# Moving TensorE filler matmuls and two weight loads in a fused recurrence and soft mixture-of-experts kernel

## The chip, the cores and the metric

The kernel runs on one core of a Trainium2 chip. Its time is that of the device, in microseconds, as the median over several runs. One execution is also profiled; the profile's own times are counted from the start of its span. The engines are named as in the profile: PE (TensorE matmuls), PEld (its weight loads), DVE (VectorE), ACT (ScalarE), POOL (GpSimd) and SP (SyncE, which only issues transfers here).

## The reference

Two stages follow each other. The first is a gated linear recurrence over 5056 steps, for 4 batches and 256 channels; the second is a soft mixture of experts with 8 experts of 4 slots each over all 20224 tokens.

```python
# first stage, x and f_logit are [4, 5056, 256]
sig = 1.0 / (1.0 + np.exp(-f_logit))
f = lower_bound + (1.0 - lower_bound) * sig
i = 1.0 - f
for t in range(S):
    h = f[:, t] * h + i[:, t] * x[:, t]
    y[:, t] = h
# second stage, x is y as [20224, 256]; phi [256, 32], w1 [8, 256, 1024], w2 [8, 1024, 256]
logits = x @ phi
d = softmax of logits over all tokens
slot_input = (d.T @ x).reshape(8, 4, 256)
slot_out[e] = np.maximum(slot_input[e] @ w1[e], 0.0) @ w2[e]
c = softmax of logits over the slots
out = c @ slot_out
```

The dispatch softmax runs over all tokens, so no expert can start before the recurrence has ended, and no output can be written before the last expert is done. The inputs are 41.4 MB of x and f_logit and 16.8 MB of weights in float32; the output is 20.7 MB.

## The kernel before

**Units.** The sequence is cut into 10 groups of 512 steps (the ninth of 448). A unit is one group of one batch, so there are 40 units, numbered so that `n // 4` is the group and `n % 4` the batch. The loop at L425 walks through them. For a unit, `load` (L174) issues the transfers of f_logit and x on SP's queue six units ahead; `gate` (L192) computes the sigmoid on ACT; `enter` (L202) multiplies it with x on POOL into `u_t`; `s_to_channels` and `u_to_channels` transpose both into PSUM on PE; `decay` (L242) makes the factor `a` on ACT; `scan` (L253) runs the recurrence on DVE; `to_tokens` (L266) transposes the result back on PE into `hp`; and `keep_tokens` copies it to `ht`, on DVE or ACT.

**Groups.** Two groups at a time, `logits` multiplies with phi, `exps` (L308) takes the exponential on ACT, `weights_to_tokens` (L315) transposes it on PE into `ep` and copies it on DVE into `et`, and `slots` (L348) accumulates the slot inputs. With blocks of eight units, the exponential of a pair of groups comes at a unit with `n % 8 == 1`, its transposes at the end of the next unit, its first `slots` at the end of the one with `n % 8 == 3`.

**The order is written by hand.** The schedule is manual (L143), so each engine executes its instructions in the order of the program text. An engine that waits holds up everything behind it on that engine.

**Fillers.** `idle` (L163) issues matmuls on PE whose result nobody reads; they write the second half of the slot bank. They stand in the loop behind `u_to_channels` (L473 to L476). `spin` (L135) does the same later on, with a weight as operand and `tail` as destination. `rs_ps`, which holds the row sums of the combining softmax, is another part of `tail`.

**Weights.** `load_w` (L128) issues one expert weight on POOL's queue, converting float32 to bfloat16: 1 MB read, 512 KB written. The first eight are `w1_sb` (L130), the others `w2_sb` (L132). `W_AT` (L141) says behind which unit's `enter` how many are issued; the issues share POOL with `enter`, in order.

**Experts and output.** After the recurrence, `sin` (the normalised slot input) goes through w1 for all experts (`hi_ps`, L559), transposes (`ht_ps`), w2 for experts 0 to 3 (L595) and for 4 to 7 (L605). Experts 4 to 7 are one block of eight matmuls each, which waits for its `w2_sb`. Between the second and third block stand the remaining row sums and `SPINS` spins (L612 to L618). Then `slot_out` (L619) is scaled on DVE, `slot_bd` made on POOL, and the output stage multiplies, scales on DVE and ACT, and stores on SP's queue.

Of the kernel before, what the change touches and what calls it, by code (L numbers as in the profile page):

```python
# [18 lines left out]
def kernel(  # L19
# [10 lines left out]
    nc = tc.nc  # L30
    B, S, D = x.shape
    E = moe_w1.shape[0]
    F = moe_w1.shape[2]
    NS = moe_phi.shape[1]
    SPE = NS // E
    P = 128
# [5 lines left out]
    n_unit = n_grp * B  # L42
# [27 lines left out]
    ident = consts.tile([P, P], BF16, name="ident")  # L70
# [13 lines left out]
    def rep_constants(b):  # L84
        blk = ident_f[ds(b * NS, NS), ds(b * NS, NS)]
        nc.gpsimd.tensor_copy(rep[ds(b * NS, NS)], blk.unsqueeze(1).broadcast_to([NS, B, NS]))
# [48 lines left out]
    def spin(dst, k, w):  # L135
        for _ in range(k):
            nc.tensor.matmul(dst[:, ds(0, w)], w1_sb[0][:, 0, :P], w1_sb[0][:, 0, :w],
                             start=True, stop=True, skip_group_check=True)

    SPINS = 28  # L140
    W_AT = {17: 1, 25: 1, 30: 1, 31: 1, 32: 1, 33: 2, 34: 1, 36: 8}  # L141
    w_next = [0]
    ctx.enter_context(tc.manual_schedule())  # L143

# [3 lines left out]
    with tc.tile_pool(name="sp2", bufs=3) as sp2, \  # L148
# [9 lines left out]
        slot_bank = pslot.tile([P, 2, D], F32, name="slot_ps")  # L158
        slot_ps = slot_bank[:, 0]

        rep_bf = rep.rearrange("p b s -> p (b s)").bitcast(BF16)

        def idle(k, first=False):  # L163
            for i in range(k):
                nc.tensor.matmul(slot_bank[:, 1], ident, rep_bf,  # L165
                                 start=first and i == 0, stop=False, skip_group_check=True)
        xs, fs, sts, uts, pss, psus, hs, hps, hts, lgs, ets = ({} for _ in range(11))

        def tokens(src, n, k):
# [22 lines left out]
        def gate(n, k=2):  # L192
            if n % 2 == 0:
                sts[n // 2] = sp2.tile([P, 2, R, D], BF16, name="s_t", tag="s_t")
            s_t, f_t = sts[n // 2][:, ds(n % 2, k)], fs[n // 2][:, ds(n % 2, k)]
            if n // B == odd:
                m = (R + R3) * D
                s_t = s_t.rearrange("p u r d -> p (u r d)")[:, :m]
                f_t = f_t.rearrange("p u r d -> p (u r d)")[:, :m]
            nc.scalar.activation(s_t, f_t, ACT.Sigmoid, scale=-1.0)  # L200
# [27 lines left out]
        def s_to_channels(n):  # L228
            if n % 2 == 0:
                pss[n // 2] = psp.tile([P, 2, P, R], F32, name="sp", tag="sp")  # L230
            to_channels(n, pss[n // 2][:, n % 2], sts[n // 2][:, n % 2],
                        sts[n // 2][:, 0, R3])
# [31 lines left out]
        SINGLE = 6  # L264
# [28 lines left out]
        def batch_of(g):  # L293
            return [g & ~1, g | 1] if g < n_grp - 2 else [g]
# [64 lines left out]
        def unit(f, m):  # L359
            if 0 <= m < n_unit:  # L360
                f(m)
# [5 lines left out]
        def batch(f, m, i):  # L367
            m -= i
            if 0 <= m < n_unit and m % B == B - 1:
                gs = batch_of(m // B)  # L370
                if m // B == gs[-1] and i < len(gs):
                    f(gs[i])
# [52 lines left out]
        for n in range(n_unit):  # L425
            if n < SINGLE - 2:
                if n:
                    unit(to_tokens, n - 1)
                    unit(u_to_channels, n + 1)
                s_to_channels(n + 2)  # L430
                if n + 3 < SINGLE:
                    gate(n + 3, 1)
                decay(n + 2, 1)
                if n + 3 == SINGLE:
                    gate(n + 3)
                if n % 2 == 0:
                    unit(load, n + AHEAD)
                unit(enter, n + 3)
                rep_constants(n)
            else:  # L440
                end = n >= n_unit - 6
                if n % 2 == 0:
                    unit(load, n + AHEAD)
                    if n == SINGLE - 2:
                        to_tokens(n - 1)
                        keep_tokens(n - 1)
                    if not end:
                        unit(gate, n + 4)
                else:
                    unit(decay, n + 1)  # L450
                    if n == n_unit - 5:
                        gate(n + 3)
                        exps(odd - 1)
                if not end and n != n_unit - 7:
                    group(exps, n - 2)

                unit(enter, n + 3)
                for _ in range(W_AT.get(n, 0)):
                    load_w(w_next[0])
                    w_next[0] += 1  # L460

                if n == n_unit - 2:
                    unit(u_to_channels, n + 1)
                if n != SINGLE - 2:
                    unit(to_tokens, n - 1)
                if n == n_unit - 2:
                    keep_tokens(n - 1)
                if n % 2 == 0:
                    unit(s_to_channels, n + 2)
                    unit(s_to_channels, n + 3)  # L470
                if n != n_unit - 2:
                    unit(u_to_channels, n + 1)
                if n in (n_unit - 5, n_unit - 4):  # L473
                    idle(4)
                elif SINGLE - 2 < n < n_unit - 4 and n % (2 * B) in (1, 2, 5, 6, 7):
                    idle(5, n == SINGLE - 1)  # L476
                if n == n_unit - 2:
                    tail = psp.tile([P, 2, G], F32, name="tail", tag="sp")
                    rs_ps = tail[:, 0, ds(0, n_grp * R * B)].rearrange(
                        "p (q b) -> p q b", b=B)  # L480
                    late_ps, odd_ps = (
                        tail[:, 1].bitcast(BF16)[:, ds(i * R * P, R * P)].rearrange(
                            "p (r s) -> p r s", r=R) for i in range(2))
                    logits(odd)
                    exps(odd)
                    slots(odd - 1)
                    spin(tail[:, 1], 1, G)
                    odd_weights()
                elif not end:
                    group(logits, n - 1)  # L490
            if n == n_unit - 1:
                logits(last, [0, 1, 2])
                late_exps([0, 1, 2])
                row_sums(0)
                late_weights([0, 1, 2], nc.scalar.copy)

            unit(scan, n)
            if n not in (SINGLE - 2, n_unit - 2):
                unit(keep_tokens, n - 1)
            if n == n_unit - 3:  # L500
                weights_to_tokens(odd - 1)
                slots(odd - 2)
            elif not n >= n_unit - 6:
                group(weights_to_tokens, n - 3)
                batch(slots, n - 4, 0)
                batch(slots, n - 4, 1)
        hid, wide = (ld.tile([P, 2, R, D], F32, name=i, tag="x_t") for i in ("hid", "wide"))
        hid = hid.rearrange("p u r d -> p (u r d)").bitcast(BF16)[:, ds(0, FC * E // 2 * NS)]
        wide = wide.rearrange("p u r d -> p (u r d)").bitcast(BF16)[:, ds(0, FC * E // 2 * P)]
# [19 lines left out]
        for o in range(DC):  # L529
            nc.tensor.matmul(sin_ps[:, o], slot_v[:, o], rep[:, 0],  # L530
                             start=True, stop=True, skip_group_check=True)

    with tc.tile_pool(name="ew", bufs=1) as ew, \
# [18 lines left out]
        for q in range(E // Q):  # L552
            hi = ew.tile([P, F], BF16, name=f"hi{q}")
            for k in range(2):
                hi_ps = (psu.tile([P, H], F32, name="hi_ps", tag="up") if q == 0 else
                         pbig.tile([P, H], F32, name="hi_ps", tag=f"hi_ps{k}"))
                for o in range(DC):
                    for j in range(Q):
                        nc.tensor.matmul(hi_ps[ds(j * NS, NS)], sin[:, o],  # L559
                                         w1_sb[q * Q + j][:, o, ds(k * H, H)],  # L560
                                         start=(o == 0), stop=(o == DC - 1),
                                         skip_group_check=True)
# [30 lines left out]
        for e in range(Q):  # L593
            for fc in range(FC):
                nc.tensor.matmul(so4_ps[ds(fc % 4 * NS, NS), :], hid[:, fc, e],  # L595
                                 w2_sb[e][:, fc],
                                 start=(e == 0 and fc < 4),
                                 stop=(e == Q - 1 and fc >= FC - 4),
                                 skip_group_check=True)
# [3 lines left out]
        for j in range(Q):  # L603
            for fc in range(FC):
                nc.tensor.matmul(so_ps, wide[:, fc, j].rearrange("p b s -> p (b s)"),  # L605
                                 w2_sb[Q + j][:, fc],
                                 start=j == 0 and fc == 0, stop=j == Q - 1 and fc == FC - 1,
                                 skip_group_check=True)
            if j == 0:
                nc.tensor.matmul(so_ps, rep2, so4, start=False, stop=False,  # L610
                                 skip_group_check=True)
            if j == 1:  # L612
                for i in range(1, len(blocks)):
                    row_sums(i)
                q = n_grp * R - 1
                spin(tail[:, 1], SPINS, NS)
                nc.vector.reciprocal(rrow[:, wide_r:q], rs_ps[:, wide_r:q])
                nc.vector.reciprocal(rrow[:, q, ds(0, B // 2)], rs_ps[:, q, ds(0, B // 2)])  # L618
        nc.vector.tensor_scalar_mul(slot_out, so_ps, rcs)  # L619
        for u in range(2):  # L620
            nc.gpsimd.tensor_scalar_mul(slot_bd[:, u], slot_out, parity[:, ds(u, 1)])  # L621
# [139 lines left out]
```

## Time and profile before

| what | value |
|---|---|
| median of 7 runs | 202.17 us (201.5 to 205.59) |
| the profiled execution's own time | 203.09 us |
| its span | 201.3 us |
| mean granted clock of PE | 0.847 |
| PE, DVE, ACT, POOL busy | 71%, 71%, 68%, 51% of the span |
| queue of SP's loads and stores | 62.13 MB, 75.7% of the 16 DMA engines' span |
| queue of POOL's weight loads | 8.42 MB written, 21.2% of the 16 DMA engines' span |
| filler matmuls, L165 | 108, 273 ns each |
| spin matmuls, L137 | 73 |

The busy shares are averages over stages that differ: up to about 130 us the recurrence, to 147 us the experts, then the output. [...] A DMA share above 1 comes from packets of one engine that overlap. GB/s counts bytes written, so a weight load shows half of what it reads.

### The profile page before, as it was taken

Reading aid. Unit: us, or ns where it says so; the run is one execution under the profiler, and the core shown is the slowest. Engines: PE = TensorE matmul, PEld = TensorE weight load, DVE = VectorE, ACT = ScalarE, POOL = GpSimd, SP = SyncE. Lnnn points to the kernel's source line nnn. Section 1 sums busy time; section 2 is a strip of 40 time slices with the busy share of each in tenths; the row PEclk is TensorE's granted clock in tenths of the full one; section 3 lists DMA queues with packets and bytes.
Section 4 is the critical chain, followed back from the end, with each engine's and each line's share of the span. In section 5 each row is a group of like instructions: output and inputs, shape, how many; then the busy total and the mean of one; then the engine's idle time right before and its main releaser. Section 6 shows DMA issues by size and latency. Waiting matters only on the chain.

```text
span 201.3 us, 3263 instructions
## 1 busy us (share of the span) xinstructions
PE 143.8 (71%) x1201; PEld 104.9 (52%) x1201; DVE 142.7 (71%) x164; ACT 137.8 (68%) x194; POOL 101.9 (51%) x76
## 2 busy tenths in 40 slices
PE   0588585895878789785988778996779999970000
PEld 0367454684676678574876666665753533320000
DVE  1669878999999979999799999351157887860000
ACT  3588676999999979899696694621047889990000
POOL 2489596865999396956968679900030000000000
PEclk9999889999999969999699999999985555555555
DMA  6999999999999999999999999999519999999994
GB/s 188 416 420 422 419 418 417 422 418 416 418 422 420 309 418 420 413 383 336 416 378 295 240 214 158 208 212 215 109 62 394 423 430 427 456 417 420 453 430 212
DMA packets 17615, 70.76 MB, mean 351 GB/s; under 512 B 2096, under 2 KB 3120, under 8 KB 16704
## 3 DMA queue, kind: packets, MB, share of 16 engines
q1 hardware_dynamic: 15120, 62.13, 75.7%
q0 software_dynamic: 2336, 8.42, 21.2%
q8 instruction: 9, 0.15, 0.3%
q14 instruction: 6, 0.05, 0.1%
q10 hardware_dynamic: 144, 0.00, 0.0%
HBM read 58.23 MB, written 20.71 MB: 392 GB/s over the span
## 4 chain that ended last, share of the span: by engine, by line
DMA 28%; PE 25%; DVE 16%; issue 9%; ACT 8%; POOL 3%; ACTq 0%; DVEq 0%; SPq 0%
DVE h L259 13%; PE op L688 11%; DMA w_sb<-in_moe_w_dram 11%; DMA f_t<-in_f_logit_dram 10%; DMA x_t<-in_x_dram 8%; PE sp L226 3%; PE hp L272 3%; PE op L639 3%; ACT a L249 3%; DVE ht L289 3%; ACT s_t L200 2%; POOL w_sb L132 2%; PE up L226 1%; ACT oc L699 1%; POOL u_t L211 1%
## 5 line engine op out<-in xcount | busy, mean ns | idle before, releaser
L211 POOL TENSOR_TENSOR u_t<-s_t,x_t 128x1024 bf16<-128x1024 bf16 (+1 forms) x39 | 82.3, 2127 | 25.6 <-ACT s_t L200 14.0
L259 DVE TENSOR_TENSOR_SCAN h<-a,h,up 128x512 bf16<-128x512 f32 (+1 forms) x72 | 86.2, 1251 | 4.9 <-PE up L226 3.1
L249 ACT ACTIVATE a<-sp,nomlb 128x1024 f32<-128x1024 bf16 (+2 forms) x46 | 43.3, 993 | 5.7 <-PE sp L226 5.4
L200 ACT ACTIVATE s_t<-f_t 128x2048 bf16<-128x2048 f32 (+2 forms) x23 | 38.5, 1675 | 9.3 <-DMA f_t<-in_f_logit_dram 9.3
L272 PE MATMUL hp<-ident_f,h 128*128 128x128 f32 (+1 forms) x160 | 30.1, 314 | 19.7 <-DVE ht L289 15.2
L272 PEld LDWEIGHTS hp<-ident_f,h 128*128 128x128 f32 (+1 forms) x160 | 23.0, 208 | 28.5 <-DVE ht L289 19.0
L226 PE MATMUL sp<-ident_f,s_t 128*128 128x128 f32 x144 | 24.1, 317 | 9.8 <-ACT s_t L200 7.8
L226 PEld LDWEIGHTS sp<-ident_f,s_t 128*128 128x128 f32 x144 | 19.6, 164 | 11.9 <-issue 6.0
L226 PE MATMUL up<-ident_f,u_t 128*128 128x128 f32 x144 | 24.6, 298 | 0.8 <-POOL u_t L211 0.8
L688 PE MATMUL op<-slot_bd,etall 64*128 64x512 bf16 x62 | 25.0, 622 | 0.2 <-ACT oc L699 0.2
L699 ACT ACTIVATE oc<-op,rrow 128x256 f32<-128x256 f32 x60 | 22.7, 488 | 2.2 <-PE op L688 1.6
L693 DVE TENSOR_TENSOR oc<-op,rrow 128x1024 f32<-128x1024 f32 x16 | 19.3, 1222 | 5.4 <-PE op L688 5.4
L226 PEld LDWEIGHTS up<-ident_f,u_t 128*128 128x128 f32 x144 | 19.0, 156 | 1.8 <-POOL u_t L211 1.2
L688 PEld LDWEIGHTS <-etall 64*128 64x128 bf16 x62 | 9.0, 155 | 14.9 <-issue 12.8
L289 DVE COPY ht<-hp 128x512 f32<-128x512 f32 (+1 forms) x22 | 14.7, 669 | 1.9 <-PE hp L272 1.9
L165 PE MATMUL slot_ps<-rep,ident 128*128 128x256 bf16 x108 | 15.4, 273 | 0.0
L633 ACT ACTIVATE ob<-op,rrow 128x256 f32<-128x256 f32 x16 | 6.3, 479 | 12.2 <-PE op L639 12.0
L289 ACT COPY ht<-hp 128x512 f32<-128x512 f32 (+1 forms) x18 | 10.5, 586 | 5.7 <-PE hp L272 5.7
L259 DVE TENSOR_TENSOR_SCAN h<-a,up 128x512 bf16<-128x512 f32 x8 | 9.3, 1210 | 2.6 <-ACT a L249 1.9
L165 PEld LDWEIGHTS <-ident 128*128 128x128 bf16 x108 | 10.6, 98 | 1.0
L621 POOL TENSOR_SCALAR slot_bd<-slot_out,parity 128x256 bf16<-128x256 bf16 x2 | 1.8, 919 | 16.9 <-DVE slot_out L619 16.9
L303 PE MATMUL lg<-h,phi 128*32 128x512 bf16 (+1 forms) x80 | 7.3, 414 | 0.0
(98 smaller groups left out, 125.3 us busy)
## 6 DMA issues: line engine op xcount, KB each, us to landing
f_t<-in_f_logit_dram SPq DMA_DIRECT2D x36, 512.0 KB, 9.9
x_t<-in_x_dram SPq DMA_DIRECT2D x36, 512.0 KB, 9.9
out_dram<-oc SPq DMA_DIRECT2D x6, 2048.0 KB, 12.7
w_sb<-in_moe_w_dram POOLq DMA_DIRECT2D x16, 512.0 KB, 10.1
out_dram<-oc SPq DMA_DIRECT2D x4, 896.0 KB, 5.2
out_dram<-ob SPq DMA_DIRECT2D x1, 2048.0 KB, 8.4
f_t<-in_f_logit_dram SPq DMA_DIRECT2D x4, 384.0 KB, 8.6
x_t<-in_x_dram SPq DMA_DIRECT2D x4, 384.0 KB, 9.0
```

Of the source, the lines that this page charges most:

```text
L165: nc.tensor.matmul(slot_bank[:, 1], ident, rep_bf, start=first and i == 0, stop=False, skip_group_check=True)
L200: nc.scalar.activation(s_t, f_t, ACT.Sigmoid, scale=-1.0)
L211: nc.gpsimd.tensor_tensor(uts[n][:, :r], s_t[:, :r], x_t[:, :r], ALU.mult)
L226: nc.tensor.transpose(ps[:, :, r], t[:, r], ident_f)
L249: nc.scalar.activation(decays[n // 2, o][:, ds(n % 2, k), :T], sp[:, ds(n % 2, k), :T, o], ACT.Identity, scale=nomlb[:, ds(o, 1)], bias=1.0)
L259: nc.vector.tensor_tensor_scan(h[:, :T, o], decays[n // 2, o][:, n % 2, :T], up[:, :T, o], hs[n - B][:, ds(used(n // B - 1) - 1, 1), o] if ...
L272: nc.tensor.transpose(hp[:n_p, r], hw[:, :n_p, r], ident_f)
L289: copy(hts[g][:n_p, b].rearrange("p r d -> p (r d)").bitcast(F32), hps.pop(n)[:n_p].rearrange("p r c -> p (r c)"))
L303: nc.tensor.matmul(lg[ds(b * NS, NS), :], phi[:, o], hs[g * B + b][:, :T, o], start=o == 0, stop=o == DC - 1, skip_group_check=True)
L688: nc.tensor.matmul(op[:, i_r].rearrange("p u d -> p (u d)"), ew[:, :, r + i_r], slot_bd[ds(j * 2 * NS, 2 * NS)].rearrange("s u d -> s (u d)"),
L693: nc.vector.tensor_tensor(ob[:, :, ds(r, k)].rearrange("p u r d -> p r u d"), op[:, ds(0, k)], scale[:, ds(r, k)].unsqueeze(3).broadcast_t ...
L699: nc.scalar.activation(ob[:, u, r + i_r], op[:, i_r, u], ACT.Copy, scale=scale[:, r + i_r, ds(u, 1)])
```

## The change

Four things change.

1. `W_AT`: at unit 34 three weights are issued instead of one, and at unit 36 six instead of eight. The order of the weights stays.
2. `idle` in the loop: the five fillers at units 10, 18, 26 and 34 are gone. Eight fillers come at the end of units 11, 19 and 27, behind `slots`. Six narrower ones (128 columns, with the identity as both operands, since `rep` is not complete there) come at unit 4. Those at units 5, 6, 7, 9, 13, 14, 15, 17, 21, 22, 23, 25, 29, 30, 31, 33, 35 and 36 stay.
3. The spins between the second and third block of L605: 14 of 128 columns instead of 28 of 32.
4. Four spins of 256 columns come between the last matmul of L605 and the output stage's first.

```diff
-    SPINS = 28
-    W_AT = {17: 1, 25: 1, 30: 1, 31: 1, 32: 1, 33: 2, 34: 1, 36: 8}
+    SPINS = 14
+    W_AT = {17: 1, 25: 1, 30: 1, 31: 1, 32: 1, 33: 2, 34: 3, 36: 6}
...
         def idle(k, first=False):
+            rhs = ident if first else rep_bf
             for i in range(k):
-                nc.tensor.matmul(slot_bank[:, 1], ident, rep_bf,
-                                 start=first and i == 0, stop=False, skip_group_check=True)
+                nc.tensor.matmul(slot_bank[:, 1, ds(0, rhs.shape[1])], ident, rhs,
+                                 start=first and i < 2, stop=False, skip_group_check=True)
...
                 if n in (n_unit - 5, n_unit - 4):
                     idle(4)
-                elif SINGLE - 2 < n < n_unit - 4 and n % (2 * B) in (1, 2, 5, 6, 7):
-                    idle(5, n == SINGLE - 1)
+                elif n == SINGLE - 2:
+                    idle(6, True)
+                elif n < n_unit - 4 and n % (2 * B) in (1, 5, 6, 7):
+                    idle(5)
...
                 batch(slots, n - 4, 1)
+                if n > 2 * B and n % (2 * B) == 3:
+                    idle(8)
...
-                spin(tail[:, 1], SPINS, NS)
+                spin(tail[:, 1], SPINS, P)
...
+        spin(tail[:, 1], 4, D)
         nc.vector.tensor_scalar_mul(slot_out, so_ps, rcs)
```

## The prediction

> **What bounds the kernel now.** I read the rows of slices first, because they show which resource is full and where it is not. Columns are fortieths of the span, 5.03 us each.
>
> ```profile
> PEclk9999889999999969999699999999985555555555
> DMA  6999999999999999999999999999519999999994
> ```
>
> The DMA engines are full from the first slice to about 144 us and again from 151 us. The holes are the start, the stretch from 143 to 151 us, and the tail. PE, DVE and ACT are hidden behind the transfers unless they stop them. So a gain must either close a hole or let the last weight land sooner. The chain of waits says which (start, length, what):
>
> ```profile
> 121.15 3.65 POOL w_sb L132 x7
> 124.80 21.24 DMA w_sb<-in_moe_w_dram
> 146.05 0.04 issue
> 146.09 1.05 PE so_ps L605 x8
> 147.14 0.03 issue
> 147.16 0.06 DVE slot_out L619
> ```
>
> The last of 16 expert weights, issued by POOL at 124.80, lands at 146.05; eight matmuls, `slot_out` and the output follow at once. Everything to the right shifts with 146.05. Next, one-microsecond windows (columns: stretch, length, busy time of PE, PEld, DVE, ACT, POOL, granted clock, DMA share, GB/s written):
>
> ```profile
> 120.00:121.00 1.00, 1.00 (x13) 1.00 (x13) 1.00 (x2) 1.00 (x2) 1.00 (x1) 1.00 1.02 205
> 121.00:122.00 1.00, 0.34 (x7) 0.18 (x4) 1.00 (x3) 0.68 (x1) 1.00 (x3) 1.00 0.86 172
> 122.00:123.00 1.00, 0.87 (x19) 0.66 (x20) 1.00 (x2) 0.00 (x0) 1.00 (x3) 1.00 0.89 115
> 123.00:124.00 1.00, 1.00 (x16) 0.79 (x17) 1.00 (x2) 0.15 (x1) 1.00 (x3) 1.00 0.86 143
> 124.00:125.00 1.00, 1.00 (x25) 0.47 (x17) 1.00 (x2) 1.00 (x3) 1.00 (x3) 1.00 1.05 188
> 125.00:126.00 1.00, 1.00 (x9) 0.94 (x8) 1.00 (x2) 0.28 (x2) 1.00 (x2) 1.00 1.02 180
> ...
> 142.00:143.00 1.00, 1.00 (x19) 1.00 (x18) 0.00 (x0) 0.00 (x0) 0.00 (x0) 1.00 1.02 205
> 143.00:144.00 1.00, 1.00 (x36) 1.00 (x36) 0.00 (x0) 0.00 (x0) 0.00 (x0) 1.00 0.48 94
> 144.00:145.00 1.00, 1.00 (x17) 0.84 (x14) 0.75 (x2) 0.00 (x0) 0.00 (x0) 1.00 0.09 16
> 145.00:146.00 1.00, 0.09 (x1) 0.00 (x0) 0.00 (x1) 0.00 (x0) 0.00 (x0) 1.00 0.04 8
> ```
>
> Two things matter. The weight stream, some 211 GB/s when it runs freely, falls to 172, 115, 143, 188 and 180 from 121 to 126 us: the queue ran dry. And after 143 us only one or two of the 16 engines still work, so the last landing belongs to the slowest one.
>
> **The weights at unit 34.** POOL's own timeline shows where they are issued (start, length, operation):
>
> ```profile
> 110.33 1.12 POOL L130 DMA_DIRECT2D w_sb<-in_moe_w_dram  x2
> 111.46 2.17 POOL L211 TENSOR_TENSOR u_t<-s_t,x_t 128x1024 bf16<-128x1024 bf16 x1
> 113.56 0.58 POOL L130 DMA_DIRECT2D w_sb<-in_moe_w_dram  x1
> 116.90 4.26 POOL L211 TENSOR_TENSOR u_t<-s_t,x_t 128x1024 bf16<-128x1024 bf16 x2 [2.77 <-issue]
> 121.11 4.29 POOL L132 DMA_DIRECT2D w_sb<-in_moe_w_dram  x8
> ```
>
> 113.56 is unit 34. Two more issues of 0.58 us end at 115.3, inside POOL's idle 2.77 us before 116.90; they delay nothing on POOL. Without that cover `enter(38)` and `enter(39)` would be 1.16 us late. At 121.11 six remain, so `hid` and `wide` are cleared 1.1 us sooner, which nobody waits for.
>
> What they do to the queue: a load's landings are recorded once per DMA engine. The eighth weight landed on the 16 engines between 121.79 and 124.19, the ninth between 125.88 and 128.82, the sixteenth between 143.17 and 146.05. From ninth to sixteenth the slowest engine takes 17.23 us for seven, **2.46 us** each. So the ninth should have cost 2.46 and cost 4.09 (first landings) to 4.63 (last): an exposed start of 1.63 to 2.17 us on every engine. With two weights, 4.92 us of work, already queued at 121, no engine runs dry before 126, and the other six are issued from 121.1 to 124.4. The slowest engine then ends at 124.19 + 8 x 2.46 = 143.87 instead of 146.05. Bounds: GB/s missing from 121 to 127 over 211 is 1.3 us (a mean over engines); the per-engine start gives 1.6 to 2.17. The last landing is what PE waits for, so I take **2.1 us**.
>
> A rule of the Trainium skill prices the same thing ("DMA: Bandwidth & Descriptors", "Anatomy of one DMA"): about 2.0 us fixed per load from GpSimd plus its bytes at 436 GB/s, here an estimate of 4.4 us for 1 MB read. By that rule taken load by load, moving a load removes nothing, since each carries its own 2.0 us. The row shows 2.46 between loads that queue up and 4.1 to 4.6 only after an empty queue. So one start goes away, not none. The same page ("Queues, rings and completion order") speaks against the change: engines alternate between queues packet by packet, so two more weights can take turns from the last x loads, the latest of which landed at 117.08. By it, up to 4.92 us on x. In the trace weights six to eight were still landing until 116.6, 119.2 and 121.7 to 124.2 on the slowest engines: the turns are already taken. I take 0.
>
> **Can PE follow?** `wide` is filled at 137.91, so `so_ps` can start at 137.95 when its weights lie ready: first eight matmuls and the `so4` one 1.2 us, then from 141.13 to 144.06 the trace has 2.93 for the next eight, the row sums and the spins, then 0.87. PE reaches the last eight at about 143.0 against 143.9 for the weight. Slack 0.9, so all of the 2.1 arrives. Against today's 146.09 that side has 3.1.
>
> **The spins.** The 28 of 32 columns start at 143.36 and the next matmul at 144.06: 0.70 us. Fourteen of 128 columns, by the nearest row (eight transposes of 128, L574: 0.58), are 1.0 us: 0.3 more, leaving slack of 0.6. `rrow` (L617) waits for the spins: from about 142.4 to 143.2, ahead of `slot_out`. Cost 0. Four spins of 256 columns behind the last `so_ps` are 4 x 0.108 (five fillers of L165 issue in 0.54) = 0.43; `slot_out` takes 147.16 to 147.64 and the first output matmul starts at 147.70. Covered at full clock but for a weight load of 0.14: 0 to 0.1, I take 0.05; at half clock 0.4.
>
> **The fillers.** Gone at units 10, 18, 26 and 34: 4 x 5 x 0.108 = 2.2 us of PE, each 0.54 ahead of the `ep` transposes. New at 11, 19 and 27: 8 x 0.108 = 0.87 behind `slots`, where PE now idles 2.1 us for DVE (69.3 to 71.4); at half clock 1.7, still inside. New at unit 4: six of 128 columns, 0.3 to 0.64 us. From 20.23 to 23.64, 68.02 to 71.43 and 91.91 to 95.32 PE was busy 1.11, 1.31 and 1.31 us of 3.41, and the next 3.41 us ran at half clock; stretches with 2.1 stayed full. 1.31 + 0.87 reaches that, so I expect the second and third dips to vanish. Each cost DVE 1.3 us (busy 1.71 of 3 in 72 to 75). But DMA was at 1.03 in them: worth **0** at the end, at most some slack behind the loads; without that cover 2.6 us.
>
> Here too a rule is weighed: "TensorE: Matmul & The Clock Gate" has PE fall to half clock after an idle window of some 3.4 us, and advises against idle gaps over about 3. By it, gaps of 2.1 us need no fillers and the drop at 149.94 would not come. The trace has drops without such gaps: before 149.94 PE was busy 2.21 of 3.42, much of it on 32 rows. If the spins moved that drop later, the price is bounded by DMA shares of 0.38 and 0.50 in 149 to 151 (the half clock covers the latter: 0.5) and by 0.82 at 155: at most 0.6. By the rule 0. With 0.43 added to some 1.0 of full-array activity the window still resembles those that fell, so I take 0.1.
>
> **Sum.** -2.1 + 0.05 - 0.1 = -2.15. The profiled execution (span 201.3) took 203.09 us and would take 200.9. The median is 0.9 lower; the same difference gives 202.17 - 2.15 = **200.0**.
>
> **Rivals.** *Part of the start stays* (0.17): packets in 122 to 128 us were slow, 12.9 engine-us in excess, 0.8 us per engine. If the burst of issues causes that, and not the empty queue, 1.3 is left: 200.9. For it: it lasts past the first load. Against: the two issues at 110.33 show none.
>
> *Hidden anyway* (0.08): if the engine that ends last never ran dry, its end is its own total, and 202.2 stays. For it: one engine is 1.2 us behind the next. Against: its ninth load shows 4.63.
>
> *Slower* (0.13): PE falls to half clock once the recurrence ends. Place: 129 to 144 us, whose 3.41 us windows now have 3.16, 3.16, 2.35, 2.54 and 2.41 busy, with work of 32 columns or 4-column row sums that may count little. Once cold it stays cold: after 149.94, 3.41 of 3.41 on 64 rows didn't bring it back. Matmuls of 8.0 us would double (L559 2.07, L574 1.38, L595 1.06, L605 3.5); less 0.6 slack that is 207.4. It decides from some 2.75 us lost, which is 0.6 of slack and 2.15 of gain. Against: the new order has less waiting and wider spins.
>
> **How the numbers follow.** Likeliest 0.62, own range 199.3 (all 2.17 and the 0.6 of clock) to 200.7; partial 0.17 to 201.6; hidden 0.08; slower 0.13. Range 199.3 to 202.2. A measurement tells 0.3%, 0.6 us, from no change: faster 0.79, same 0.08, slower 0.13.
>
> **What would show it.** Right: DMA share above 1.0 through 121 to 126 us; last weight near 144; last `so_ps` waiting under 1 us for it; no half clock behind units 11, 19 and 27; output stage 54 us long as now. Wrong: a hole of the same size elsewhere, one engine still landing at 146, `enter(38)` waiting for x, or half clock before the output.

## The result

| | before | after |
|---|---|---|
| median, with the runs of this comparison | 202.97 us (64 runs) | 201.06 us (27 runs) |
| ratio, 95% interval | | 0.9916 [0.9897, 0.9935] |
| profiled execution, its span | 203.09, 201.3 us | 201.46, 199.7 us |
| last weight lands | 146.05 | 144.05 |
| last x lands | 117.08 | 122.25 |
| `slot_out` starts | 147.16 | 145.84 |
| from there to the end | 54.14 | 53.86 |

The kernel is 0.84% faster. The medians count every run, while the ratios leave out runs more than 1.5% above the fastest of their kernel (5 of the 64 here), so the two differ a little. The time lies inside the forecast range and 1.1 us above the forecast of 200.0. Of the 1.6 us that the span lost, 1.32 come before `slot_out` and 0.28 behind it; the forecast was 2.1 and 0.05.

Lines L164 to L474 of before stand one higher in the changed kernel, `so_ps` of the last experts is L610 and `slot_out` L625. First the page's rows of slices:

```profile
PEclk9999879999999999999999969999995555555555
DMA  5999999999999999999999999999529999999994
```

The dips of the clock in slices 14 and 19 are gone; a new one stands in slice 23, after PE had sat idle for 2.66 us from 113.46. The hole between weights and output is still there. The one-microsecond windows (PE, PEld, DVE, ACT, POOL, clock, DMA share, GB/s) at the place where the queue ran dry:

```profile
121.00:122.00 1.00, 0.88 (x12) 0.72 (x10) 1.00 (x1) 0.66 (x1) 0.00 (x0) 1.00 1.12 229
122.00:123.00 1.00, 0.00 (x0) 0.00 (x0) 1.00 (x3) 0.00 (x0) 0.59 (x1) 1.00 1.02 205
123.00:124.00 1.00, 0.62 (x16) 0.33 (x16) 1.00 (x2) 0.00 (x0) 1.00 (x1) 1.00 1.04 209
124.00:125.00 1.00, 0.40 (x4) 0.40 (x5) 1.00 (x2) 0.00 (x0) 1.00 (x2) 1.00 1.09 217
...
142.00:143.00 1.00, 1.00 (x20) 1.00 (x20) 0.00 (x0) 0.00 (x0) 0.00 (x0) 1.00 0.41 78
143.00:144.00 1.00, 1.00 (x21) 0.99 (x20) 0.00 (x0) 0.00 (x0) 0.00 (x0) 1.00 0.04 8
```

DMA stays full, and the weights end two microseconds sooner. But PE is now idle at 122 and busy without a break at 143: it no longer waits for the last weight. The chain of waits says so (start, length, what):

```profile
141.92 1.30 PE tail L337 x23
143.23 0.02 PE tail L340
143.25 0.80 PE tail L137 x14
144.06 1.76 PE so_ps L610 x16
145.82 0.03 issue
145.84 0.06 DVE slot_out L625
```

Sixteen `so_ps` matmuls run in one go; no landing of a weight stands before them. What made PE late is on POOL's timeline:

```profile
110.26 0.58 POOL L130 DMA_DIRECT2D w_sb<-in_moe_w_dram  x1
110.83 1.07 POOL L132 DMA_DIRECT2D w_sb<-in_moe_w_dram  x2
118.58 2.14 POOL L212 TENSOR_TENSOR u_t<-s_t,x_t 128x1024 bf16<-128x1024 bf16 x1 [6.68 <-DMA x_t<-in_x_dram]
122.41 2.14 POOL L212 TENSOR_TENSOR u_t<-s_t,x_t 128x1024 bf16<-128x1024 bf16 x1 [1.68 <-DMA x_t<-in_x_dram]
124.49 3.23 POOL L132 DMA_DIRECT2D w_sb<-in_moe_w_dram  x6
```

`enter(38)` waits 6.68 us for x and `enter(39)` another 1.68. Before, POOL waited there for 2.77 us and not for x. And unit 34 comes at 110.26 instead of 113.56. So two questions: which part of the change carries the gain, and which part holds x back.

### The profile page after: what moved, and what is told of

Its sections match the earlier page's. It is cut to its first block, busy times and chain, and to the rows that moved or that the text cites. A ratio compares the mean times of both kernels' runs of the same rounds, so it can differ in the third digit from the quotient of the medians.

```text
span 199.7 us, 3263 instructions
## 1 busy us (share of the span) xinstructions
PE 143.7 (72%) x1201; PEld 104.8 (52%) x1201; DVE 142.3 (71%) x164; ACT 137.7 (69%) x194; POOL 102.0 (51%) x76
## 4 chain that ended last, share of the span: by engine, by line
DMA 42%; PE 25%; ACT 10%; issue 5%; DVE 5%; POOL 2%; SPq 0%; ACTq 0%; DVEq 0%; POOLq 0%
DMA x_t<-in_x_dram 26%; DMA f_t<-in_f_logit_dram 16%; PE op L694 11%; ACT s_t L201 3%; ACT a L250 3%; DVE h L260 3%; POOL u_t L212 2%; PE op L645 2%; PE so_ps L610 2%; ACT oc L705 1%; PE tail L137 1%; PE hp L273 1%; PE tail L337 1%; PE hi_ps L564 1%; ACT L201 1%
## 5 line engine op out<-in xcount | busy, mean ns | idle before, releaser
L273 PE MATMUL hp<-ident_f,h 128*128 128x128 f32 (+1 forms) x160 | 29.6, 309 | 16.1 <-DVE ht L290 12.1
L227 PE MATMUL sp<-ident_f,s_t 128*128 128x128 f32 x144 | 23.1, 308 | 13.1 <-ACT s_t L201 11.1
L227 PEld LDWEIGHTS sp<-ident_f,s_t 128*128 128x128 f32 x144 | 18.6, 158 | 15.1 <-issue 6.0
L694 PE MATMUL op<-slot_bd,etall 64*128 64x512 bf16 x62 | 24.5, 609 | 0.2
L166 PEld LDWEIGHTS <-ident 128*128 128x128 bf16 x118 | 11.6, 101 | 1.8 <-issue 0.6
```

Source lines behind the costliest of these rows:

```text
L166: nc.tensor.matmul(slot_bank[:, 1, ds(0, rhs.shape[1])], ident, rhs, start=first and i < 2, stop=False, skip_group_check=True)
L227: nc.tensor.transpose(ps[:, :, r], t[:, r], ident_f)
L273: nc.tensor.transpose(hp[:n_p, r], hw[:, :n_p, r], ident_f)
L694: nc.tensor.matmul(op[:, i_r].rearrange("p u d -> p (u d)"), ew[:, :, r + i_r], slot_bd[ds(j * 2 * NS, 2 * NS)].rearrange("s u d -> s (u d)"),
```

## The experiments

**Theory A**: the weights carry the gain, by removing one exposed start. x is late because the moved fillers made the units, and with them the weights of units 30 to 34, 3 us earlier, so that these weights share the engines with the last x loads. **Theory B**: the two extra weights themselves hold x back. **Theory C**: fillers and clock carry the gain. The runs of before lie beside each group: 202.87 us for the first four, 202.74 for the next, 202.9 for the last.

### The weights alone

```diff
-    W_AT = {17: 1, 25: 1, 30: 1, 31: 1, 32: 1, 33: 2, 34: 1, 36: 8}
+    W_AT = {17: 1, 25: 1, 30: 1, 31: 1, 32: 1, 33: 2, 34: 3, 36: 6}
```

> The kernel before with the change of W_AT alone. Theory A (the weights carry the gain, and the x loads of units 38 and 39 are late in the changed kernel because the fillers made POOL issue the weights of units 30 to 34 some 3 us sooner): 1.3 to 2.1 us faster than before; the ninth weight lands 2.5 us behind the eighth on the slowest engine; the last x lands by 118, as before; the wait of enter(38) for x stays under 1 us; the last weight lands near 144. Theory B (the two extra weights themselves take the turns of the last x loads): the last x lands near 122 here too, enter(38) waits some 6 us for it, gain about 1.5. Theory C (fillers and clock carry the gain): within 0.3 us of before.

Measured: 201.0 us, ratio 0.9956 [0.9921, 0.9991]. The ninth weight lands 2.4 us behind the eighth (124.5, 126.9), the last at 144.1. The last x lands at 118.9. POOL's timeline of this kernel:

```profile
112.51 0.57 POOL L130 DMA_DIRECT2D w_sb<-in_moe_w_dram  x1
113.08 1.07 POOL L132 DMA_DIRECT2D w_sb<-in_moe_w_dram  x2
115.84 2.15 POOL L211 TENSOR_TENSOR u_t<-s_t,x_t 128x1024 bf16<-128x1024 bf16 x1 [1.69 <-ACT s_t L200]
119.04 2.17 POOL L211 TENSOR_TENSOR u_t<-s_t,x_t 128x1024 bf16<-128x1024 bf16 x1 [1.06 <-DMA x_t<-in_x_dram]
```

With the same two extra weights, `enter(38)` doesn't wait for x at all and `enter(39)` 1.06 us. B falls: in two more kernels further down, with these weights and the old places of the fillers, the last x lands at 117.1 and 116.3. C falls as the main cause, for this part alone reaches the median of the whole change. By the ratios it is 0.4% against 0.8%, with intervals that overlap, so what the other parts add is not told apart here.

### One weight instead of two

```diff
-    W_AT = {17: 1, 25: 1, 30: 1, 31: 1, 32: 1, 33: 2, 34: 1, 36: 8}
+    W_AT = {17: 1, 25: 1, 30: 1, 31: 1, 32: 1, 33: 2, 34: 2, 36: 7}
```

> As before, with two weights at unit 34 and seven at unit 36: one load moved instead of two. If the gain is the removal of one exposed start, one load in the queue (2.46 us of work, from 121.8 to 124.3) is enough to cover the 1.3 us until the next issue takes effect, and the gain equals that of two loads within 0.5 us. If the gain is proportional to the loads moved, it is half.

Measured: 201.5 us, ratio 0.9928 [0.9892, 0.9965], inside 0.5 us of two. The ninth weight lands 2.4 us behind the eighth (125.4, 127.9) and the DMA share is at 1.0 or above throughout:

```profile
124.00:125.00 1.00, 0.76 (x18) 0.55 (x19) 1.00 (x2) 0.00 (x0) 1.00 (x3) 1.00 1.05 213
125.00:126.00 1.00, 1.00 (x12) 0.86 (x14) 1.00 (x2) 0.03 (x1) 1.00 (x3) 1.00 1.13 205
126.00:127.00 1.00, 1.00 (x25) 0.52 (x17) 1.00 (x2) 1.00 (x3) 1.00 (x3) 1.00 1.04 201
127.00:128.00 1.00, 1.00 (x8) 0.82 (x8) 1.00 (x2) 0.28 (x3) 1.00 (x2) 1.00 1.00 201
```

The profiled execution was the slowest of its eleven, 203.11 us, with six stretches of half clock before the output, late units and the last weight at 145.2. So it shows the closed gap, and the time rests on the other executions. One load in the queue closes the gap: what was gained is one start, not a time per load moved. The difference of 0.5 us between medians is not told apart by these intervals.

### The fillers alone

```diff
-                elif SINGLE - 2 < n < n_unit - 4 and n % (2 * B) in (1, 2, 5, 6, 7):
-                    idle(5, n == SINGLE - 1)
+                elif n == SINGLE - 2:
+                    idle(6, True)
+                elif n < n_unit - 4 and n % (2 * B) in (1, 5, 6, 7):
+                    idle(5)
...
+                if n > 2 * B and n % (2 * B) == 3:
+                    idle(8)
```

> The kernel before with the fillers of the loop moved, W_AT and spins unchanged. Theory A: the half clock behind units 11 and 19 is gone, the weights of units 30 to 34 are issued some 3 us sooner, the last x lands near 122, enter(39) ends near 124.5, the last eight weights are issued only then, onto an empty queue, and the kernel is 0.5 to 3 us slower than before. Theory B: the last x lands by 118 and the time is that of before within 0.5 us. Theory C: 1 to 2 us faster.

Measured: 204.38 us, ratio 1.0079 [1.003, 1.0127]: **slower**. POOL's timeline, and then the windows:

```profile
110.45 0.57 POOL L130 DMA_DIRECT2D w_sb<-in_moe_w_dram  x1
118.72 2.14 POOL L212 TENSOR_TENSOR u_t<-s_t,x_t 128x1024 bf16<-128x1024 bf16 x1 [7.70 <-DMA x_t<-in_x_dram]
122.54 2.14 POOL L212 TENSOR_TENSOR u_t<-s_t,x_t 128x1024 bf16<-128x1024 bf16 x1 [1.68 <-DMA x_t<-in_x_dram]
124.63 4.29 POOL L132 DMA_DIRECT2D w_sb<-in_moe_w_dram  x8
```

```profile
122.00:123.00 1.00, 0.21 (x4) 0.05 (x1) 1.00 (x3) 0.00 (x0) 0.46 (x1) 1.00 0.45 90
123.00:124.00 1.00, 0.54 (x16) 0.33 (x16) 1.00 (x2) 0.00 (x0) 1.00 (x1) 1.00 0.17 33
124.00:125.00 1.00, 0.34 (x6) 0.27 (x3) 1.00 (x2) 0.00 (x0) 1.00 (x2) 1.00 0.00 0
125.00:126.00 1.00, 1.00 (x12) 0.80 (x14) 1.00 (x2) 0.09 (x1) 1.00 (x3) 1.00 0.51 33
```

Without any extra weight, x is as late as in the changed kernel (122.4) and `enter(38)` waits 7.7 us. The eight weights stand behind `enter(39)` in POOL's order, so they too are 3.5 us late, and now all 16 engines stop: the share reaches 0.00. The last weight lands at 147.8, `slot_out` starts at 149.38.

### The fillers with later weights

```diff
-    W_AT = {17: 1, 25: 1, 30: 1, 31: 1, 32: 1, 33: 2, 34: 1, 36: 8}
+    W_AT = {17: 1, 25: 1, 32: 2, 33: 2, 34: 2, 36: 8}
```

> The kernel with the fillers alone moved (204.38 us), and the weights of units 30 and 31 issued later: W_AT is {17: 1, 25: 1, 32: 2, 33: 2, 34: 2, 36: 8}, so again eight up to unit 34. Theory A (the fillers make the weights come sooner than the last x loads, which then share their engines' turns): the last x lands 4 us or more before 122.4, enter(38) no longer waits 7.7 us for it, the last eight weights are issued before the queue runs dry, slot_out starts some 3 us before 149.4, and the time falls to 200.5 to 202. Rival (the fillers themselves, on PE, are what costs): the time stays near 204.4.

Measured: 201.29 us, ratio 0.9941 [0.9905, 0.9976]. The last x lands at 113.9, `enter(38)` no longer waits for it, and the weights of unit 36 begin at 117.58 instead of 124.63; `slot_out` starts at 144.87:

```profile
113.38 4.25 POOL L212 TENSOR_TENSOR u_t<-s_t,x_t 128x1024 bf16<-128x1024 bf16 x2 [2.23 <-issue]
117.58 3.23 POOL L132 DMA_DIRECT2D w_sb<-in_moe_w_dram  x6
```

PE's fillers are the same, so they are not what costs. That is A shown from both sides: what held x back was the weights that the quicker units issued among the last x loads.

### The changed kernel with later weights

```diff
-    W_AT = {17: 1, 25: 1, 30: 1, 31: 1, 32: 1, 33: 2, 34: 3, 36: 6}
+    W_AT = {17: 1, 25: 1, 32: 2, 33: 3, 34: 3, 36: 6}
```

> The changed kernel with the same weights later: W_AT is {17: 1, 25: 1, 32: 2, 33: 3, 34: 3, 36: 6}. Theory A: the last x lands by 116 instead of 122.3, the wait of enter(38) for it falls from 6.7 to under 2 us, the last weight lands at 144 as in the changed kernel, PE waits for it again, slot_out starts at 145.0 instead of 145.8: 200.2 us, 0.5 to 0.9 under the changed kernel. If the lateness of x has nothing to do with the weights ahead of it, 201.1. If the weight queue now starts too late, the last weight lands behind 145 and the time is above 201.5.

Measured: 200.21 us, ratio 0.9872 [0.9836, 0.9909]; last x 114.1, last weight 143.6, `slot_out` 144.75. POOL's timeline:

```profile
110.52 0.57 POOL L130 DMA_DIRECT2D w_sb<-in_moe_w_dram  x1
111.09 1.07 POOL L132 DMA_DIRECT2D w_sb<-in_moe_w_dram  x2
113.33 4.25 POOL L212 TENSOR_TENSOR u_t<-s_t,x_t 128x1024 bf16<-128x1024 bf16 x2 [1.17 <-issue]
117.53 2.27 POOL L132 DMA_DIRECT2D w_sb<-in_moe_w_dram  x4
```

The wait for x is gone, and PE waits 0.94 us for the last weight again, as forecast for the change itself. Six runs are few, so it ran again beside the changed kernel.

> The changed kernel once more, beside the next: 201.1, the last x behind 120, enter(38) waiting for it.

> The changed kernel with the later weights once more: 200.2, 0.4% under the changed kernel, the last x by 115 and no wait of enter(38) for it.

Measured, on one chip: 200.79 us for the changed kernel, 0.9919 [0.9886, 0.9951]; 200.59 with the later weights, 0.992 [0.9885, 0.9954]. The traces differ as expected (last x 121.9 and 114.0; `enter(38)` waiting 6.21 us and not at all; `slot_out` 145.53 and 144.96), but the times do not. In this execution the output stage took 54.0 us against 53.7, with DMA shares of 0.41 and 0.59 at its start against 0.75 and 0.99. So the late x is shown, and an advantage of removing it is not.

### The spins

```diff
-    SPINS = 28
+    SPINS = 14
...
-                spin(tail[:, 1], SPINS, NS)
+                spin(tail[:, 1], SPINS, P)
...
+        spin(tail[:, 1], 4, D)
```

> The kernel before with 14 spins of 128 columns in place of 28 of 32, and four of 256 columns behind the last block. All theories: between 0.4 us faster (the half clock before the output comes one window later and the first stores are earlier) and 0.1 us slower. If it is over 0.6 us faster, the spins carry a good part of the gain.

Measured: 203.2 us, ratio 1.0001 [0.9962, 1.004]: no change. In its trace two things cancel. `slot_out` starts at 146.18, 1.0 us sooner than before, and from there to the end it takes 55.2 us, 1.0 us longer. The first came about ahead of any changed spin: with the weights and loop fillers of before, the ninth weight lands 2.84 us behind the eighth (126.73, 123.89) where it was 4.63, and the last at 145.07. So the exposed start seems to differ from execution to execution. The second is taken up next.

> The kernel before with W_AT and both changes of the spins, without the moved fillers. The kernel with W_AT alone (201.0) had half clock from 141.6 to 145.0 in its profile, with so_ps slowed to 0.42 us a matmul at worst. If the wider spins hold the clock there, slot_out starts 0.5 us sooner than 145.63 and the time is 200.5; if that dip was chance, 201.0 within 0.3.

Weights and spins, fillers as before: 201.68 us, ratio 0.9952 [0.9921, 0.9983]. `slot_out` started at 144.49, over 1 us sooner than with the weights alone (there the half clock from 141.6 to 145.0 had slowed `so_ps`), and yet the time was not better. The windows show where it went:

```profile
147.00:148.00 1.00, 0.93 (x7) 0.54 (x5) 1.00 (x3) 1.00 (x4) 0.00 (x0) 1.00 0.66 206
148.00:149.00 1.00, 0.94 (x4) 0.56 (x5) 0.86 (x2) 1.00 (x4) 0.00 (x0) 1.00 0.16 51
149.00:150.00 1.00, 1.00 (x5) 0.34 (x3) 1.00 (x2) 1.00 (x4) 0.00 (x0) 0.68 0.23 81
150.00:151.00 1.00, 1.00 (x4) 0.39 (x3) 1.00 (x1) 1.00 (x4) 0.00 (x0) 0.50 1.05 404
```

The output's transfers all but stop for two microseconds just after they have begun. SP's timeline has one store whose issue took 2.00 us, where 0.35 to 0.9 is usual in the changed kernel:

```profile
147.32 2.00 SPq L666 DMA_DIRECT2D out_dram<-ob  x1
```

The last 16 KB of the instruction queue were moved at 147.18. In the kernel with the spins alone, the same load is at 148.70, the first store at 147.80, and one issue takes 1.66 us. In before, the changed kernel and the one with the weights alone it starts at 147.22, 145.02 and 145.2 and is over ahead of the first store, at 148.79, 147.46 and 147.26. The two kernels with the hole have 3243 instructions, those others 3263.

> The kernel before with W_AT and the spins changed (201.68), and ten more fillers at units 9 to 17, two each, so that PE's program is as long as in the kernel before and in the changed one (3263 instructions in all instead of 3243). If the hole at the first stores (DMA share 0.66, 0.16, 0.23 from 147 to 150, one store's issue 2.0 us long while the last 16 KB of the instruction queue is moved) comes from the place at which that load falls, the load moves ahead of the first store, the stage from slot_out to the end is 54 us instead of 55.5, and the time is 200.3 to 200.9. If the hole has another cause, 201.7 and 55.5 stay.

The edit puts the ten matmuls and ten weight loads back:

```diff
-                    idle(5, n == SINGLE - 1)
+                    idle(7 if n in (9, 13, 14, 15, 17) else 5, n == SINGLE - 1)
```

Measured: 200.45 us, ratio 0.9903 [0.9867, 0.994]. The load moved to 144.73, the first store came at 146.46, and from `slot_out` to the end it took 54.1 us instead of 55.5. The windows no longer have the hole:

```profile
147.00:148.00 1.00, 1.00 (x9) 0.87 (x8) 1.00 (x2) 0.99 (x3) 0.33 (x1) 0.81 0.38 131
148.00:149.00 1.00, 1.00 (x5) 0.37 (x4) 0.94 (x2) 1.00 (x4) 0.00 (x0) 0.50 0.84 313
149.00:150.00 1.00, 1.00 (x4) 0.31 (x3) 0.49 (x1) 0.67 (x2) 0.00 (x0) 0.50 1.08 416
```

With ten added fillers the kernel is 1.2 us quicker between medians, though the two intervals just overlap, and in the traces the stage behind `slot_out`, where the hole was, is 1.4 us shorter. What moved there is the instruction load. The clock is not the cause: here the half clock begins at 147.6, sooner than in any of these kernels but one.

> The changed kernel without the four spins of 256 columns behind the last block. If they carry part of the 0.3 us by which the output stage got shorter (53.9 from slot_out to the end, 54.1 before): 201.2 to 201.5, with the half clock within 3 us of slot_out. If not: 201.0 to 201.1, and slot_out to the end stays 53.9.

The changed kernel without its last four spins:

```diff
-        spin(tail[:, 1], 4, D)
```

Measured: 201.47 us, ratio 0.9959 [0.9929, 0.9989]; from `slot_out` to the end 53.9 us, half clock 4.8 us behind `slot_out`. With the spins it came 4.4 us behind (150.25), and 5.7 us in the second trace of the changed kernel, so that they hold the clock is not shown. A worth of 0.4 us can't be told from none.

### Later weights without the fillers

The kernel with the weights, the spins and the ten padding fillers (200.45 us), its loop fillers in their old places, but with the later `W_AT`:

```diff
-    W_AT = {17: 1, 25: 1, 30: 1, 31: 1, 32: 1, 33: 2, 34: 3, 36: 6}
+    W_AT = {17: 1, 25: 1, 32: 2, 33: 3, 34: 3, 36: 6}
```

> The same with the later weights, W_AT {17: 1, 25: 1, 32: 2, 33: 3, 34: 3, 36: 6}. If the later weights are what counts and the fillers' place is worth nothing at the end, 200.2 to 200.6. If the fillers' pace is needed as well (the weights of unit 32 come some 3 us later without it, on an empty queue, or the recurrence ends too late), over 200.8.

Measured: 202.53 us, ratio 0.9986 [0.9946, 1.0026]: the gain is gone. The weights of unit 32 are issued at 106.83 here and not at 102.51. Most of the x loads are done by then (the very last lands at 108.8), and the engines run short of work before the first of these weights arrives:

```profile
106.00:107.00 1.00, 0.25 (x2) 0.25 (x3) 1.00 (x3) 1.00 (x1) 1.00 (x2) 1.00 0.99 406
107.00:108.00 1.00, 1.00 (x10) 1.00 (x10) 1.00 (x2) 0.54 (x2) 0.94 (x2) 1.00 0.42 172
108.00:109.00 1.00, 1.00 (x14) 0.70 (x14) 0.92 (x2) 0.65 (x2) 0.26 (x1) 1.00 0.93 102
```

The last weight lands at 146.0, as before the change. So the same `W_AT` is good or bad by the pace of the units, and the fillers set that pace.

## Why the prediction was right, and where it was off

**The exposed start: right in kind, sized from one execution.** Forecast: last landing at 143.87, 2.46 us a load, no hole at 121 to 126. Measured: 144.05, 2.4 between eighth and ninth, DMA shares of 1.02 and more. In all eleven traces with more than eight weights issued before unit 36, or with unit 36 early enough, the ninth comes 2.44 or 2.45 us behind the eighth. The run with one weight shows that it is the empty queue that cost, and so the rival of a start that stays in part is out; the slow packets that spoke for it went as well (344 ns each on POOL's queue from 122 to 128 us before, 296 after). The price of 2.0 us per load from the Trainium skill ("DMA: Bandwidth & Descriptors", "Anatomy of one DMA") fits the 1.63 to 2.17 us found in before, for the first load after an empty queue alone. But the 2.1 us were one execution's: in the trace with the spins alone, at the same weights, the start was 0.4 us on the slowest engine. That fits a gain below 2.1; how the start spreads over executions is not known from two traces.

Two readings in the forecast were off, without weight for it: from 143 to 144 us half of the engines still worked (DMA share 0.48), one or two only after that, and the landings from 116.6 to 124.2 are those of the fifth to the eighth weight.

**No turns taken from x: the step that failed.** The text said "the turns are already taken. I take 0" for x, and held up 4.92 us as the price by the rule of the same page ("Queues, rings and completion order") that engines alternate between queues. The last x landed 5.17 us later, and `enter(38)` waited for it, one of the forecast's own signs of being wrong. That weights issued ahead of x hold it back, as the rule would have it, is what the runs with later weights show; that turns go packet by packet no run here shows. But the two extra weights were not the cause, so the nearness of 5.17 to 4.92 is chance: with them alone x was at 118.9, with the fillers alone at 122.4. What failed was to read the landings of the trace of before as if the weights stayed at their places in it.

**The fillers, "worth 0 at the end": wrong, and by sign.** Their effect on the clock was as forecast: no half clock behind units 11 and 19. All 14 traces agree: the seven with the fillers moved have none between 60 and 100 us and issue the weights of unit 34 from 110.0 to 110.8; of the seven with the old places, those with one such stretch issue them from 112.5 to 113.1, those with two from 113.6 to 115.7. But the forecast stopped at DVE. Quicker units also mean that POOL issues unit 34 at 110.26 instead of 113.56, with weights ahead of x. Alone that costs 1.5 us. In the change the two weights in the queue cover it: weights queued by then go on until 129.2 while `enter(39)` is late, so most of the cost is hidden (`slot_out` 0.8 us later than forecast, against 2.2 later than before with the fillers alone), and what is left shows on PE.

**PE's slack of 0.6 to 0.9: used up.** With x late, `sin` starts at 134.69 instead of 132.78, 1.9 us. The slack was smaller, so `slot_out` came 0.8 us later than the 145.06 that 147.16 less 2.1 gives. This is the difference between forecast and result before `slot_out`.

**Spins: right.** Fourteen took 0.78 us from the first to the next matmul (1.0 forecast). The first output matmul came 0.54 us behind `slot_out`'s start, as before: cost 0, not 0.05. The 0.28 us behind `slot_out` is larger than the 0.1 for the clock, inside its bound of 0.6. It goes with the clock: half clock came 4.4 us behind `slot_out` instead of 2.8, and the twelve traces without the hole broadly follow the same order (last section). What moved the clock stays open; the run without the last spins doesn't show that they did.

**The base.** The forecast started from 202.17, the median of seven runs; over 64 it was 202.97. Against that the gain is 1.9 us between medians, 1.7 by the ratio, and 2.15 was forecast. That the time fell inside the range is in part luck: 201.06 lies above the 199.3 to 200.7 of the likeliest case, in the part of the range that stood there for a start that stays in part, which did not occur.

The slower rival, half clock through the experts, did not occur in the changed kernel. Four other traces have one such stretch of 3.4 us among the experts. With the weights alone it ran from 141.6 to 145.0, and sixteen `so_ps` matmuls took 3.44 us instead of 1.91: the mechanism exists, for 3.4 us at a time and not for the whole stage.

## What to carry to other kernels

Where transfers fill the span, look for the moment at which a queue runs dry, and keep one load waiting in it: the start of the next is then hidden. Ask of every speedup off the path which transfers it will issue earlier, and whose turns these take; a due time counted in units moves when the units do. Change the two together: here the fillers alone lost 1.5 us and the later weights alone lost the whole gain.

## What the runs showed of the hardware that was not expected

- An instruction load and the first stores can hold each other up. Where 16 KB of the instruction queue were moved during the first stores, the load took 1.8 (and 1.6) us instead of 0.9 to 1.3, one issue on SP took 2.0 (and 1.66) us, and the output stage was 55.5 (and 55.2) us long instead of 53.7 to 54.8. Twenty more instructions on PE, far earlier, moved the load and removed the delay. Two kernels with and twelve traces without fit this, with one run made to test it; which engine's instructions the load carried is not known.
- The output stage is shorter the longer the clock stays up behind `slot_out`. In the twelve traces without that hole, half clock 1.9 to 2.8 us behind `slot_out` goes with a stage of 54.1 to 54.8 us (five traces), 4.1 to 5.7 us with 53.7 to 54.0 (seven). Whether the changed spins make it late is not shown: six of those seven have the wide spins, but so has one of the five.
- The exposed start seems to differ from execution to execution: at the same weights and loop fillers, the load behind the empty queue came 4.63 us behind the last in one trace and 2.84 in another.
